# The second phase's output tiles: added in DRAM by accumulating transfers of GpSimd's queue, moved out of PSUM by ScalarE

## The chip, the cores and the metric

The kernel runs on one core of a Trainium2 chip. A time is the device time of one execution in microseconds (us); the median of several executions is given. Engines are named as in the profile: PE (TensorE), PEld (its weight loads), DVE (VectorE), ACT (ScalarE), POOL (GpSimd), SP (the queue from which the transfers are issued). L and a number is a line of the kernel's file.

## What is computed

Linear attention with an exponential feature map, then a gated feed-forward layer over its 4608 tokens (8 batches of 576), all in float32:

```python
def phi(x):
    proj = np.einsum('bhsd,df->bhsf', x, w_phi)
    proj = proj - np.max(np.abs(proj), axis=-1, keepdims=True)
    return np.concatenate([np.exp(proj), np.exp(-proj)], axis=-1)
q_p, k_p = phi(q), phi(k)
num = q_p @ (k_p^T v); den = q_p . sum_s k_p + 1e-06
x = (num / den), heads side by side          # 4608 x 512
gate = 1 / (1 + exp(-(x @ w_gate)))          # 512 -> 1536
out = (gate * (x @ w_val)) @ w_out           # 1536 -> 512
```

## The kernel before

**Two phases.** The 1536 hidden columns are twelve groups of 128. The first phase computes the attention, pair of heads by pair of heads (`attend`), and beside it the feed-forward layer's first four groups (`first_js`), whose output is a partial sum of every output tile of 128 tokens by 512 columns. The second phase does the other eight groups in two passes of four groups each, over six chunks (`dc`) of 768 tokens: twelve calls of `pass_over`. The three partial sums of a tile (first phase, first pass, second pass) have to be added.

**A chunk of a pass** is two stages on PE. The first is 28 products of six matmuls of 384 columns (`group`, line 1229, 168 matmuls) in tiles of the PSUM ring `bank`, which has five. Four groups of seven products follow one another; each group begins with a product of which ACT makes a copy (line 1247), and DVE adds the further products onto that copy (line 1242), which frees their banks. The second stage is 72 matmuls of 512 columns (`out_part`, line 1311) into six output tiles `acc`, twelve to a tile, in the PSUM ring `gate`, which has three banks. We call the six T0 to T5. The first two or three of them are done half and half in turn. Meanwhile ACT and DVE split the next chunk's input blocks into a high and a low part (lines 1187 and 1191), from loads of line 1167.

**An output tile's end** is `finish` (lines 1129 to 1145). SP loads the partial sum so far from a scratch tensor in DRAM into the ring `r_y1` of three buffers (line 1134), DVE adds it to `acc` from PSUM into a tile `y` (line 1139), and SP stores `y` (line 1143). The ring `r_y` has two buffers, so the sum of a tile waits until the store of the tile two before has landed. The partial sums lie in `yscr` (written by the first phase at line 1000, read in the first pass), `y2scr` (written by the first pass, read in the second), and the second pass writes `out`.

**What sets the order.** Every operation is first an entry of a plan (`Plan.op`) with an engine, an estimated length and a rank; `Plan.run` simulates the engines and lists the entries by their simulated start. The instructions are written in that order, and each engine executes its own strictly in it. An instruction at the head of its queue that waits for a buffer keeps all later ones of that engine waiting.

Of the kernel before, what the change touches and what calls it, by code (L numbers as in the profile page):

```python
# [8 lines left out]
F32 = mybir.dt.float32  # L9
# [4 lines left out]
ALU = mybir.AluOpType  # L14
# [6 lines left out]
P = 128  # L21
NP = H // 2
DM = H * D
# [4 lines left out]
CW = 512  # L28
NCH = NT // CW
# [6 lines left out]
DC = 2 * HT  # L36
# [112 lines left out]
class Plan:  # L149


    SWITCH = 0.15
    NEAR = {"PE": 0.3, "DVE": 0.05, "ACT": 0.05, "SP": 0.0, "X": 0.0}
    SAME = {"PE": 0.0, "DVE": 0.12, "ACT": 0.13, "SP": 0.0, "X": 0.0}
    RATE = 0.26

    def __init__(self):
# [21 lines left out]
    def run(self):  # L179
        free = dict.fromkeys(self.NEAR, 0.0)  # L180
        ready = {e: [] for e in free}
        mode, wire = None, 0.0
        for o in self.ops:
            if not o.wait:
                ready[o.eng].append(o)

        def pick(b, taken):
            best, when = None, None
            for ring in b.rings:
                for s in ring:  # L190
                    t = s.at()
                    if t is None or any(s.hits(x) for x in taken):
                        continue
                    if best is None or t < when:
                        best, when = s, t
            return best

        def start(o):
            t = max(o.ready, free[o.eng])
            if o.eng == "PE" and mode not in (None, o.mode[0]):  # L200
                t = max(o.ready, free[o.eng] + self.SWITCH)
            taken = []
            for b in o.bufs:
                if b.rings and b.slot is None:
                    s = pick(b, taken)
                    if s is None:
                        return None
                    taken.append(s)
                    t = max(t, s.at())
            return t  # L210

        order, left = [], len(self.ops)
        while left:
            best = None
            for e, cs in ready.items():
                ts = [(t, o) for o in cs if (t := start(o)) is not None]
                if not ts:
                    continue
                first = min(t for t, _ in ts) + self.NEAR[e]

                def key(x):
                    t, o = x
                    off = e == "PE" and mode not in (None, o.mode[0])
                    return o.rank + STICK * off, t

                t, o = min((x for x in ts if x[0] <= first), key=key)
                if best is None or t < best[0]:
                    best = t, o
            if best is None:
                raise RuntimeError(f"no work can go on: {[(o.eng, o.rank) for c in ready.values() for o in c][:40]} {left}")  # L230
            t, o = best
            ready[o.eng].remove(o)
            for b in o.bufs:
                if b.rings and b.slot is None:
                    b.slot = pick(b, ())
                    b.slot.take()
            free[o.eng] = t + o.busy
            if o.eng == "SP":
                wire = max(wire, t) + o.lag * self.RATE ** -1 * 1e-6
                end = wire + 2.0  # L240
            else:
                end = t + o.busy + o.lag
            if o.eng == "PE":
                mode = o.mode[-1]
            for cells in o.opens:
                n = len(cells.free)
                cells.free, cells.taken = [end] * n, [False] * n
            for b in o.bufs:
                b.left -= 1
                b.end = max(b.end, end)  # L250
                if not b.left and b.slot:
                    b.slot.give(b.end)
            for n in o.then:
                n.wait -= 1
                if n.eng != o.eng or o.eng == "SP":
                    at = end + n.slack
                else:
                    at = t + o.busy + self.SAME[o.eng]
                n.ready = max(n.ready, at)
                if not n.wait:  # L260
                    ready[n.eng].append(n)
            order.append((t, o))
            left -= 1
        return order
# [3 lines left out]
def attention_moe(  # L268
# [9 lines left out]
    nc = tc.nc  # L278
    vec, act = nc.vector, nc.scalar
# [3 lines left out]
    dram = ctx.enter_context(tc.tile_pool(name="dram", bufs=1, space=DRAM))  # L283
# [42 lines left out]
    nc.sync.dma_start(wk, w_phi)  # L326

    xscr = [dram.tile([P, NC4, CW], F32, tag=f"xs{c}", name=f"xs{c}") for c in range(NCH)]
    yscr = [dram.tile([4, P, DM], F32, tag=f"ys{c}", name=f"ys{c}") for c in range(NCH)]
    y2scr = [dram.tile([4, P, DM], F32, tag=f"yt{c}", name=f"yt{c}") for c in range(NCH)]  # L330
    wscr = [dram.tile([2, P, DM], F32, tag=f"wo{j}", name=f"wo{j}") for j in range(NJ)]
    gscr = {
        (n, m): dram.tile([2, P, 7 * 2 * P], F32, tag=f"g{n}{m}", name=f"g{n}{m}")
# [18 lines left out]
    r_top = x.ring(2, DM, U32)  # L352
    x = low()
    r_X = x.ring(14, 2 * HT)
    r_y1 = x.ring(3, DM)
    r_h = x.ring(8, 2 * HT)
    r_wo = x.ring(8, DM)
    x = high()
# [25 lines left out]
    def dve(n, fn, reads, writes, rank, k=1.0, after=()):  # L384
        return plan.op("DVE", 0.07 + n / 960 / k, 0.16, fn, reads, writes, rank, after=after)

    def on_act(n, fn, reads, writes, rank, after=()):
        return plan.op("ACT", 0.08 + n / 1200, 0.17, fn, reads, writes, rank, after=after)

    def sp(size, fn, reads, writes, rank, after=()):  # L390
        return plan.op("SP", 0.06, size, fn, reads, writes, rank, after=after)

    def head(hd):
        return slice(hd * D, hd * D + D)
# [580 lines left out]
    def first_js(c, r, step):  # L975

        banks = [r_g] if c < NCH - 2 else [r_g, r_a]
        hs = []
        for i in range(JA):
            hs.append(gate(c, i, r + 2 * i * step, banks, c == 0))  # L980
        for t in range(CW // P):
            acc, y = Buf(banks, [P, DM]), Buf([r_y], [P, DM])

            def go(t=t, acc=acc):
                for i in range(JA):
                    mm_out(acc, t, hs[i], i, i == 0, i == JA - 1)

            pe(
                "f", 0.685 * JA, go,
                [x for h in hs for x in h] + [x for i in range(JA) for x in weights[i][1]],  # L990
                [acc], r + (2 * JA + t) * step, 0.3,
            )
            on_act(
                DM, lambda y=y, acc=acc: act.activation(
                    y(), acc(), AF.Copy, scale=0.5 if c < LATE else 1.0
                ),
                [acc], [y], -90.0,
            )
            sp(
                256 << 10, lambda t=t, y=y: nc.sync.dma_start(yscr[c][t], y()),  # L1000
                [y], [(ymark[c], t)], r,
            )

# [122 lines left out]
        weigh(j, 2, r, False, wh, wl, slice(0, DM), None, after)  # L1126
        return wh, wl

    def finish(T, acc, src, mark, dst, dmark, r):

        c, t = divmod(T, CW // P)
        y1, y = Buf([r_y1], [P, DM]), Buf([r_y], [P, DM])
        sp(
            256 << 10, lambda: nc.sync.dma_start(y1().bitcast(F32), src[c][t]),
            [(mark[c], t)], [y1], r - 12.0, [done],
        )
        dve(
            DM,
            lambda: vec.tensor_tensor(y(), acc(), y1().bitcast(F32), op=ALU.add),  # L1139
            [acc, y1], [y], -90.0,  # L1140
        )
        sp(
            256 << 10, lambda: nc.sync.dma_start(dst(c, t), y()), [y],
            [(dmark[c], t)] if dmark else [], r,
        )

    prior, taken, outs = [fed], [], []
# [143 lines left out]
                [t, (hh, h)], [(hl, h)], z,  # L1291
            )

    def pass_over(ns, dc, r, ws, wo, src, mark, dst, dmark):

        x = x_blocks(dc, r - XLEAD)
        hs = []
# [4 lines left out]
        for T in range(DC // P):  # L1302
            acc = Buf([r_g], [P, DM])
            h, o = divmod(T * P, HT)
            for i, n in enumerate(ns):
# [13 lines left out]
                    + [y for j in pair(n) for y in wo[j]],  # L1319
                    [acc], r + 29.2 + 1.4 * T + 0.7 * i, 0.3,  # L1320
                ))
            finish(dc * (DC // P) + T, acc, src, mark, dst, dmark, r + 29.2 + 2.8 * T)

    def final(c, t):
        return out[c * CW + t * P : c * CW + t * P + P, :]

    SPAN = 46.0
    y2mark = [Buf() for _ in range(NCH)]
    ws, wo, marks = {}, {}, {}
    for n in range(2):  # L1330
        r = base - 30.0 + 30.0 * n
# [7 lines left out]
        wo[j] = fetched([r_wo], DM, wscr[j], marks[j], start - 20.0, [done])  # L1339
    for dc in range(NDC):  # L1340
        r = start + SPAN * dc
        pass_over(
            (0, 1), dc, r, ws, wo, yscr, ymark, lambda c, t: y2scr[c][t], y2mark
        )
        if dc < 4:
            n, m = 2 + dc // 2, dc % 2
            mark = marks[n, m] = Buf()
            kept(combine(n, m, r + KEEP, [r_stage], [done]), gscr[n, m], mark, r + KEEP)
            j = JA + 4 + dc
            mark = marks[j] = Buf()  # L1350
            kept(out_weight(j, r + KEEP + 10.0, [r_swo], [done]), wscr[j], mark, r + KEEP)
# [4 lines left out]
    for j in (*pair(2), *pair(3)):  # L1356
        wo[j] = fetched([r_wo], DM, wscr[j], marks[j], start + 10.0)
    for dc in range(NDC):
        pass_over((2, 3), dc, start + SPAN * dc, ws, wo, y2scr, y2mark, final, None)
    order = plan.run()  # L1360
    for _, o in sorted(order, key=lambda x: x[0]):
        o.fn()
# [58 lines left out]
```

## Time and profile before

| | before |
|---|---|
| median of 3 runs | 1160.05 us (1159.93 to 1161.06) |
| the profiled execution | 1160.85 us, of it 1158.9 us span of the core |
| granted PE clock | 0.998 |
| busy: PE, PEld, DVE, ACT | 1142.8, 939.5, 933.3, 583.0 us |
| bytes read from and written to DRAM | 120.06 MB, 49.42 MB |
| DVE's sums of output tiles, line 1139 | 72, 683 ns each (median) |
| transfers of 256 KB that carry partial sums and output | 36 `ys` stores, 36 `ys` loads, 36 `yt` stores, 36 `yt` loads, 36 `out` stores |

The views of the profile that are used below: the chain of work that ended last, followed back from the end (start, length, engine and line of each link); tables of stretches (busy time of each engine between two times, then PE's granted clock, the share of time in which the DMA engines were busy, and GB/s); a timeline of instructions (start, length, engine, line, output and inputs, and in brackets how long the engine had been idle and what released it); and lists of one line's instructions. SPq is SP's queue, where the time is that of issuing a transfer, not of its landing. Times count from the span's start.

### The profile page before, as it was taken

Reading aid. Unit: us, or ns where it says so; the run is one execution under the profiler, and the core shown is the slowest. Engines: PE = TensorE matmul, PEld = TensorE weight load, DVE = VectorE, ACT = ScalarE, POOL = GpSimd, SP = SyncE. Lnnn points to the kernel's source line nnn. Section 1 sums busy time; section 2 is a strip of 40 time slices with the busy share of each in tenths; the row PEclk is TensorE's granted clock in tenths of the full one; section 3 lists DMA queues with packets and bytes.
Section 4 is the critical chain, followed back from the end, with each engine's and each line's share of the span. In section 5 each row is a group of like instructions: output and inputs, shape, how many; then the busy total and the mean of one; then the engine's idle time right before and its main releaser. Section 6 shows DMA issues by size and latency. Waiting matters only on the chain.

```text
span 1158.9 us, 22323 instructions
## 1 busy us (share of the span) xinstructions
PE 1142.8 (99%) x8796; PEld 939.5 (81%) x8796; DVE 933.3 (81%) x1793; ACT 583.0 (50%) x1115; POOL 0.7 (0%) x6
## 2 busy tenths in 40 slices
PE   8999999999999999999999999999999999999998
PEld 6666566766676677678889999999999999999997
DVE  6999989888878878847897999988767757757764
ACT  6867776666656666635553444352332333323421
POOL 0000000000000000000000000000000000000000
PEclk9999999999999999999999999999999999999999
DMA  6764554344424443226526656545447433225122
GB/s 237 226 220 127 152 168 123 121 129 137 137 87 153 121 137 122 70 79 209 173 101 211 206 178 223 187 141 186 154 173 286 141 106 123 78 88 163 56 95 82
DMA packets 99441, 171.08 MB, mean 148 GB/s; under 512 B 18825, under 2 KB 43529, under 8 KB 99337
## 3 DMA queue, kind: packets, MB, share of 16 engines
q1 hardware_dynamic: 99336, 169.66, 45.7%
q8 instruction: 69, 1.13, 0.4%
q14 instruction: 36, 0.29, 0.1%
HBM read 120.06 MB, written 49.42 MB: 146 GB/s over the span
## 4 chain that ended last, share of the span: by engine, by line
PE 84%; DVE 7%; DMA 6%; ACT 2%; issue 1%; SPq 1%; DVEq 0%
PE bank L1229 30%; PE gate L1311 17%; PE gate L914 11%; PE gate L971 6%; PE bank L621 4%; PE bank L663 3%; PE bank L914 3%; DMA rb<-den 3%; PE bank L432 2%; PE bank L681 2%; DMA den<-dn 2%; PE bank L537 1%; DVE d L587 1%; PE bank L971 1%; PE bank L635 1%; PE bank L647 1%
## 5 line engine op out<-in xcount | busy, mean ns | idle before, releaser
L1229 PE MATMUL bank<-low,high 128*128 128x384 f32 x2016 | 351.8, 336 | 0.0
L1229 PEld LDWEIGHTS bank<-low,high 128*128 128x128 f32 x2016 | 349.8, 188 | 1.1
L1311 PE MATMUL gate<-low 128*128 128x512 f32 x864 | 198.4, 389 | 0.0
L1311 PEld LDWEIGHTS gate<-low 128*128 128x128 f32 x864 | 162.0, 188 | 33.2
L914 PE MATMUL gate<-low 128*128 128x512 f32 x696 | 165.7, 393 | 1.2 <-ACT flat L949 0.6
L914 PEld LDWEIGHTS gate<-low 128*128 128x128 f32 x696 | 128.6, 188 | 29.7 <-issue 1.2
L479 ACT ACTIVATE ek<-ek 128x512 f32<-128x512 f32 (+1 forms) x192 | 96.6, 526 | 27.3 <-DVE ek L467 25.9
L1242 DVE TENSOR_TENSOR more<-more,bank 128x384 f32<-128x384 f32 x111 | 61.1, 551 | 40.8 <-PE bank L1229 40.3
L971 PE MATMUL gate<-low 128*128 128x512 f32 x384 | 92.3, 394 | 0.0
L971 PEld LDWEIGHTS gate<-low 128*128 128x128 f32 x384 | 70.8, 188 | 15.1 <-issue 1.0
L621 PE MATMUL bank<-ek,vin 128*32 128x256 f32 x1240 | 74.5, 386 | 4.4 <-ACT d L545 3.8
L621 PEld LDWEIGHTS bank<-ek,vin 128*32 128x32 f32 x1240 | 37.8, 110 | 46.2 <-issue 11.0
L1139 DVE TENSOR_TENSOR flat<-gate,low 128x512 f32<-128x512 f32 x72 | 49.3, 685 | 23.3 <-PE gate L1311 11.7
L438 DVE TENSOR_REDUCE mk<-bank 128x4 f32<-128x512 f32 (+1 forms) x92 | 49.0, 552 | 21.3 <-PE bank L432 16.9
L1242 DVE TENSOR_TENSOR flat<-flat,bank 128x384 f32<-128x384 f32 x75 | 41.3, 551 | 29.3 <-PE bank L1229 29.1
L1187 ACT CAST low<-more 128x768 fp32r<-128x768 f32 x36 | 30.1, 836 | 61.1 <-DVE more L1178 60.8
L467 DVE TENSOR_TENSOR ek<-bank,mk 128x512 f32<-128x512 f32 (+1 forms) x92 | 48.2, 550 | 0.6 <-ACT d L550 0.2
L1267 ACT ACTIVATE more<-more 128x384 f32<-128x384 f32 x38 | 20.0, 525 | 57.1 <-DVE more L1242 56.9
L938 ACT CAST low<-flat 128x512 fp32r<-128x512 f32 x36 | 22.3, 620 | 51.5 <-DVE flat L963 44.9
L1284 ACT CAST low<-more 128x384 fp32r<-128x384 f32 x50 | 24.7, 513 | 46.6 <-DVE more L1280 46.6
L590 ACT ACTIVATE eq<-d 128x1152 f32<-128x1152 f32 x29 | 33.9, 1168 | 24.8 <-DVE d L587 24.4
L432 PE MATMUL bank<-wk,kin 64*128 64x128 f32 x496 | 38.7, 289 | 4.6 <-DMA kin<-k 4.3
(184 smaller groups left out, 1700.1 us busy)
## 6 DMA issues: line engine op xcount, KB each, us to landing
flat<-w_moe SPq DMA_DIRECT2D x36, 512.0 KB
low<-xs SPq DMA_DIRECT2D x46, 256.0 KB
kin<-k SPq DMA_DIRECT2D x32, 320.0 KB
qin<-q SPq DMA_DIRECT2D x32, 320.0 KB
vin<-v SPq DMA_DIRECT2D x32, 320.0 KB
ys<-flat SPq DMA_DIRECT2D x36, 256.0 KB
low<-ys SPq DMA_DIRECT2D x36, 256.0 KB
yt<-flat SPq DMA_DIRECT2D x36, 256.0 KB
```

Of the source, the lines that this page charges most:

```text
L432: nc.tensor.matmul(pk[hd]()[:, t, :], x()[head(hd), t * P : t * P + P], wk[head(hd), :], start=True, stop=True,)
L438: vec.tensor_reduce(mx, pk, axis=AX.X, op=ALU.max, apply_absolute_value=True)
L467: vec.tensor_tensor(ek[g]()[:, :, F:], src, mk[g]()[:, :ns].unsqueeze(2).broadcast_to([P, ns, F]), op=ALU.subtract,)
L479: lambda g=g, sg=sg: act.activation(ek[g]()[:, :, sg * F : sg * F + F], ek[g]()[:, :, F:], AF.Exp, scale=1.0 - 2.0 * sg,),
L621: nc.tensor.matmul(o_[o : o + Q, : 2 * F], vx()[:, 2 * t + hd, o % D : o % D + Q], (e0, e1)[hd][:, t, :] if t < 4 else e2[:, 0, :], start= ...
L663: nc.tensor.matmul(nm()[o : o + Q, :], w()[:, sg, o : o + Q], es[sg]()[:, o // D, cs], start=sg == 0, stop=sg == 1, tile_position=(0, o),)
L914: nc.tensor.matmul(o(), a()[:, ws], x(), start=cc + n == 0, stop=cc == NC4 - 1 and n == 2,)
L971: nc.tensor.matmul(acc(), a()[:, ts], w(), start=first and i == 0, stop=last and i == 2)
L1139: lambda: vec.tensor_tensor(y(), acc(), y1().bitcast(F32), op=ALU.add),
L1229: nc.tensor.matmul(o()[:, :HT], s()[:, ws], y()[:, cc, :], start=first and cc + i_ == 0, stop=cc + i_ == 3, skip_group_check=not first,)
L1242: lambda: vec.tensor_tensor(o(), p(), q()[:, :HT], op=ALU.add),
L1311: nc.tensor.matmul(acc(), s()[:, h, o : o + P], w(), start=i + e + k_ == 0, stop=i + e + k_ == 4,)
```

## The change

The scratch tensors `yscr` and `y2scr` and the ring `r_y1` are gone. The first phase stores its partial sums straight into `out`. In the second phase ACT copies each output tile from PSUM to `y`, and a transfer issued by POOL adds `y` onto the rows of `out` in DRAM. The plan gets POOL as an engine, with an estimated 1.0 us per issue and a landing estimated in the same manner as for SP's transfers.

```diff
-    yscr = [dram.tile([4, P, DM], F32, ...) for c in range(NCH)]
-    y2scr = [dram.tile([4, P, DM], F32, ...) for c in range(NCH)]
...
-    r_y1 = x.ring(3, DM)
...
+    def rows(c, t):
+        return out[c * CW + t * P : c * CW + t * P + P, :]
...
-                256 << 10, lambda t=t, y=y: nc.sync.dma_start(yscr[c][t], y()),
+                256 << 10, lambda t=t, y=y: nc.sync.dma_start(rows(c, t), y()),
...
-    def finish(T, acc, src, mark, dst, dmark, r):
+    def finish(T, acc, r):
         c, t = divmod(T, CW // P)
-        y1, y = Buf([r_y1], [P, DM]), Buf([r_y], [P, DM])
-        sp(
-            256 << 10, lambda: nc.sync.dma_start(y1().bitcast(F32), src[c][t]),
-            [(mark[c], t)], [y1], r - 12.0, [done],
-        )
-        dve(
-            DM,
-            lambda: vec.tensor_tensor(y(), acc(), y1().bitcast(F32), op=ALU.add),
-            [acc, y1], [y], -90.0,
-        )
-        sp(
-            256 << 10, lambda: nc.sync.dma_start(dst(c, t), y()), [y],
-            [(dmark[c], t)] if dmark else [], r,
-        )
+        y = Buf([r_y], [P, DM])
+        on_act(DM, lambda: act.copy(y(), acc()), [acc], [y], -90.0)
+        plan.op(
+            "POOL", 1.0, 256 << 10,
+            lambda: nc.gpsimd.dma_start(rows(c, t), y(), accum_op=ALU.add),
+            [y], [(ymark[c], t)], r,
+        )
```

Where the instructions stand after it:

**ACT, the end of the last chunk.** Of before, the last rows of ACT's queue (a copy of a group's first product, sigmoids at line 1267, and the casts of the hidden values at line 1284):

```order
991 L1267 ACTIVATE more<-more 128x384
992 L1267 ACTIVATE flat<-flat 128x384
993 L1247 COPY flat<-bank_204 128x384
994 L1284 CAST low<-flat 128x384
995 L1284 CAST low<-more 128x384 x2
996 L1284 CAST low<-flat 128x384
997 L1378 UNCONDITIONAL_BRANCH
```

Now (the same lines are 1260, 1240 and 1277; line 1133 is the new copy from the ring `gate` to a `y` tile):

```order
1077 L1240 COPY flat<-bank_186 128x384
1078 L1277 CAST low<-flat 128x384
1079 L1277 CAST low<-more 128x384
1080 L1277 CAST low<-flat 128x384
1081 L1277 CAST low<-more 128x384
1082 L1133 COPY flat<-gate_195 128x512
1083 L1133 COPY flat<-gate_188 128x512
1084 L1133 COPY flat<-gate_201 128x512
1085 L1133 COPY flat<-gate_195 128x512
1086 L1133 COPY flat<-gate_188 128x512
1087 L1133 COPY flat<-gate_201 128x512
1088 L1365 UNCONDITIONAL_BRANCH
```

The six copies T0 to T5 stand behind everything else of ACT's. In most other chunks the next row behind T5 is the copy of the next chunk's first product; that is so in the chunk before this one, where the casts of line 1180 (before: 1187) are the splits of the next chunk's input:

```order
1059 L1180 CAST low<-more 128x768
1060 L1133 COPY flat<-gate_201 128x512
1061 L1180 CAST low<-more 128x768
1062 L1133 COPY flat<-gate_195 128x512
1063 L1133 COPY flat<-gate_188 128x512
1064 L1133 COPY flat<-gate_201 128x512
1065 L1240 COPY more<-bank_174 128x384
1066 L1260 ACTIVATE flat<-flat 128x384
1067 L1260 ACTIVATE flat<-bank_174 128x384
```

All six tiles of a chunk have moved from DVE's queue into ACT's, and the last three of them stand together ahead of the next chunk's first work there.

**PE, where the first pass ends.** This is the one place of all 6536 matmuls at which PE's order changes. Before, T5 of the first pass's last chunk (`gate_219`) stood behind four products of the next pass:

```order
1418 L1311 MATMUL gate_213<-low 128x512 x12
1419 L1311 MATMUL gate_206<-low 128x512 x12
1420 L1229 MATMUL bank_192<-low,high 128x384 x6
1421 L1229 MATMUL bank_180<-low,high 128x384 x6
1422 L1229 MATMUL bank_204<-low,high 128x384 x6
1423 L1229 MATMUL bank_194<-low,high 128x384 x6
1424 L1311 MATMUL gate_219<-low 128x512 x12
1425 L1229 MATMUL bank_192<-low,high 128x384 x6
```

Now it stands behind three (`gate_201`; lines 1304 and 1222 are before's 1311 and 1229):

```order
1418 L1304 MATMUL gate_195<-low 128x512 x12
1419 L1304 MATMUL gate_188<-low 128x512 x12
1420 L1222 MATMUL bank_174<-low,high 128x384 x6
1421 L1222 MATMUL bank_162<-low,high 128x384 x6
1422 L1222 MATMUL bank_186<-low,high 128x384 x6
1423 L1304 MATMUL gate_201<-low 128x512 x12
1424 L1222 MATMUL bank_176<-low,high 128x384 x6
```

One product has moved behind T5; number, size and everything else of PE's order are as they were.

**SP and POOL, the end.** Before, SP's last rows mixed the loads of the partial sums with the stores:

```order
545 L1134 DMA low<-yt_114 128x512
546 L1143 DMA out<-flat 128x512
547 L1134 DMA low<-yt_114 128x512
548 L1143 DMA out<-flat 128x512 x4
549 L1378 UNCONDITIONAL_BRANCH
```

Now all 72 accumulating transfers are POOL's, and POOL has nothing else to do by then:

```order
9 L1136 DMA out<-flat 128x512 x72
10 L1365 UNCONDITIONAL_BRANCH
```

SP's queue is 144 transfers shorter (72 loads and 72 stores) and now ends with the loads of the last chunk's input.

More of the change, by code (lines that the diff above doesn't have):

```diff
@@ L152 @@
     SWITCH = 0.15
-    NEAR = {"PE": 0.3, "DVE": 0.05, "ACT": 0.05, "SP": 0.0, "X": 0.0}
-    SAME = {"PE": 0.0, "DVE": 0.12, "ACT": 0.13, "SP": 0.0, "X": 0.0}
+    NEAR = {"PE": 0.3, "DVE": 0.05, "ACT": 0.05, "SP": 0.0, "POOL": 0.0, "X": 0.0}
+    SAME = {"PE": 0.0, "DVE": 0.12, "ACT": 0.13, "SP": 0.0, "POOL": 0.0, "X": 0.0}
     RATE = 0.26
@@ L237, in run @@
             free[o.eng] = t + o.busy
-            if o.eng == "SP":
+            if o.eng in ("SP", "POOL"):
                 wire = max(wire, t) + o.lag * self.RATE ** -1 * 1e-6
@@ L254, in run @@
                 n.wait -= 1
-                if n.eng != o.eng or o.eng == "SP":
+                if n.eng != o.eng or o.eng in ("SP", "POOL"):
                     at = end + n.slack
@@ L328, in attention_moe @@
     xscr = [dram.tile([P, NC4, CW], F32, tag=f"xs{c}", name=f"xs{c}") for c in range(NCH)]
-    yscr = [dram.tile([4, P, DM], F32, tag=f"ys{c}", name=f"ys{c}") for c in range(NCH)]
-    y2scr = [dram.tile([4, P, DM], F32, tag=f"yt{c}", name=f"yt{c}") for c in range(NCH)]
     wscr = [dram.tile([2, P, DM], F32, tag=f"wo{j}", name=f"wo{j}") for j in range(NJ)]
@@ L1292, in valued, with pass_over @@
             )
-    def pass_over(ns, dc, r, ws, wo, src, mark, dst, dmark):
+    def pass_over(ns, dc, r, ws, wo):
         x = x_blocks(dc, r - XLEAD)
@@ L1321, in pass_over @@
                 ))
-            finish(dc * (DC // P) + T, acc, src, mark, dst, dmark, r + 29.2 + 2.8 * T)
-    def final(c, t):
-        return out[c * CW + t * P : c * CW + t * P + P, :]
+            finish(dc * (DC // P) + T, acc, r + 29.2 + 2.8 * T)
     SPAN = 46.0
-    y2mark = [Buf() for _ in range(NCH)]
     ws, wo, marks = {}, {}, {}
@@ L1341, in attention_moe @@
         r = start + SPAN * dc
-        pass_over(
-            (0, 1), dc, r, ws, wo, yscr, ymark, lambda c, t: y2scr[c][t], y2mark
-        )
+        pass_over((0, 1), dc, r, ws, wo)
         if dc < 4:
@@ L1358, in attention_moe @@
     for dc in range(NDC):
-        pass_over((2, 3), dc, start + SPAN * dc, ws, wo, y2scr, y2mark, final, None)
+        pass_over((2, 3), dc, start + SPAN * dc, ws, wo)
     order = plan.run()
```

## The prediction

> **What bounds the kernel now.** The chain of work that ended last comes first: start, length, and the engine and line of each link. It is PE without a break from 511.98 us on; its last links are these.
>
> ```profile
> 1018.77 29.12 PE bank L1229 x168
> 1047.90 16.36 PE gate L1311 x72
> 1064.26 29.12 PE bank L1229 x168
> 1093.38 16.36 PE gate L1311 x72
> 1109.73 29.12 PE bank L1229 x168
> 1138.86 16.37 PE gate L1311 x72
> ```
>
> Each link begins where the one before ends, and a chunk is 29.12 + 16.36 = 45.48 us every time. The table of stretches says what stands beside it (PE, PEld, DVE, ACT, POOL busy, then clock, DMA share, GB/s):
>
> ```profile
> 654.90:700.40 45.50, 45.50 (x242) 42.66 (x242) 44.97 (x86) 21.30 (x40) 0.00 (x0) 1.00 0.65 216
> 1018.80:1064.30 45.50, 45.50 (x242) 42.66 (x242) 31.73 (x53) 15.02 (x27) 0.00 (x0) 1.00 0.33 101
> 1109.70:1155.30 45.60, 45.52 (x241) 42.32 (x239) 22.78 (x43) 9.53 (x20) 0.00 (x0) 1.00 0.22 69
> 1155.30:1158.90 3.60, 0.00 (x0) 0.00 (x0) 0.65 (x1) 0.00 (x0) 0.00 (x0) 0.80 0.19 73
> ```
>
> PE is busy for the whole of each stretch at full clock, even in the first, where DVE works 44.97 of 45.50 us. DVE's load costs PE nothing. The second phase is as long as its matmuls, plus 3.6 us behind the last of them. That tail is the only part that can shrink. It is this (timeline; in brackets what released the instruction):
>
> ```profile
> 1141.04 0.55 DVE L1288 TENSOR_TENSOR low<-flat,low 128x384 fp32r<-128x384 f32 x1
> 1143.01 0.69 DVE L1139 TENSOR_TENSOR flat<-gate,low 128x512 f32<-128x512 f32 x1 [1.43 <-PE gate L1311]
> 1143.73 0.33 SPq L1134 DMA_DIRECT2D low<-yt  x1
> 1144.11 0.42 SPq L1143 DMA_DIRECT2D out<-flat  x1
> 1144.37 0.69 DVE L1139 TENSOR_TENSOR flat<-gate,low 128x512 f32<-128x512 f32 x1 [0.67 <-PE gate L1311]
> ...
> 1147.44 0.69 DVE L1139 TENSOR_TENSOR flat<-gate,low 128x512 f32<-128x512 f32 x1 [2.37 <-DMA out<-flat]
> ...
> 1149.88 0.69 DVE L1139 TENSOR_TENSOR flat<-gate,low 128x512 f32<-128x512 f32 x1 [1.75 <-PE gate L1311]
> 1152.53 0.69 DVE L1139 TENSOR_TENSOR flat<-gate,low 128x512 f32<-128x512 f32 x1 [1.97 <-PE gate L1311]
> 1155.25 0.69 DVE L1139 TENSOR_TENSOR flat<-gate,low 128x512 f32<-128x512 f32 x1 [2.03 <-PE gate L1311]
> 1155.97 0.33 SPq L1143 DMA_DIRECT2D out<-flat  x1
> ```
>
> These are T0 to T5 of the last chunk. PE has T0 ready at 1143.01, T1 at 1144.37, T3 at 1149.88, T4 at 1152.53, T5 at 1155.25. T2 waits for T0's buffer: a store. T5's sum ends at 1155.94, and its store lands with the span's end at 1158.9, 2.96 us later.
>
> **What the change takes away.** 72 sums of DVE and 144 of SP's transfers:
>
> ```profile
> L1139 DVE TENSOR_TENSOR flat<-gate,low x72: 678/683/693, 644.4 to 1155.3; 128x512 f32<-128x512 f32 x72
> L994 ACT ACTIVATE flat<-gate x32: 576/597/627, 101.3 to 608.6; 128x512 f32<-128x512 f32 x32
> ```
>
> 72 x 0.683 = 49 us of DVE's time go. None of it is on the chain, so I count it as nothing. ACT gets 72 copies from PSUM. The nearest operation is line 994, the same size from the same ring: 72 x 0.6 = 43 us, 3.6 us per chunk where ACT has at least 45.5 - 21.3 = 24 us free. Nothing again, and what is late next behind DVE is still PE. SP's issues and loads hide beside PE now; their going frees nothing PE waits for. One product of PE moves behind T5 where the passes meet: same work, no gap before, nothing. The first phase's engines keep their order, its stores only change their address: nothing. Were PE's cover gone there, each store would cost what SP pays to issue it, a third of a microsecond.
>
> **What it adds: the landing of an accumulating transfer.** Let L be the time from the end of a tile's copy until its `y` buffer is free again, or at the end until the run is over. No transfer of POOL, and none that adds, is in the trace, so L is bounded. Below: it reads `y` and writes `out` as a store does, and reads `out` besides, so it is not cheaper than a store. For a store in this chunk, T0's sum ends at 1143.70 and its buffer is free at 1147.44; 0.38 us of that is SP issuing a load first, so 3.36 us. At the end it is 2.96. Two more rows say that stores behind a busy queue take the same:
>
> ```profile
> 1060.13 1.43 SPq L1143 DMA_DIRECT2D out<-flat  x2
> 1063.56 0.69 DVE L1139 TENSOR_TENSOR flat<-gate,low 128x512 f32<-128x512 f32 x1 [1.49 <-DMA out<-flat]
> ```
>
> That is 3.43 us from issue to release. Above: a whole load of `out` would come first, then the store. The chain of work has a wait on loads of 256 KB:
>
> ```profile
> 214.54 4.06 DMA low<-xs
> ```
>
> 4.06 us on top gives 7.42 in the chunk and 7.02 at the end. I take half of that load on top, 2.03: the read of `out` should overlap that of `y` but not the write, and what POOL spends on issuing is unknown and can only add. So L is 5.4 us in the chunk and 5.0 at the end. I choose the middle because no row is nearer to one end.
>
> **The sum.** A copy takes 0.6 us. `y` has two buffers, so T3's copy waits for T1's transfer and T5's for T3's. T1's copy ends at 1144.37 + 0.6 = 1144.97. T3's starts at the later of 1149.88 and 1144.97 + 5.4 = 1150.37. T5's starts at the later of 1155.25 and 1150.97 + 5.4 = 1156.37, ends at 1156.97, and lands 5.0 later: 1161.97. Against 1158.9 that is +3.1 us. In general the end is the later of 1155.85 + L(end) and 1146.17 + 2 L(chunk) + L(end): beyond L of 4.8 each microsecond counts three times. With L at the plain store the end is 1158.8, -0.1 us; with the whole load on top it is 1168.0, +9.1.
>
> **Does PE wait in the other eleven chunks?** ACT waits for `y` with the next chunk's first copy queued behind it, for which DVE's additions and then PE's banks wait. A row of before shows how much room there is (a chunk whose first product starts at 1018.61):
>
> ```profile
> 1019.85 0.48 ACT L1247 COPY flat<-bank 128x384 f32<-128x384 f32 x1 [4.65 <-PE bank L1229]
> 1020.96 0.56 DVE L1242 TENSOR_TENSOR flat<-flat,bank 128x384 f32<-128x384 f32 x1 [1.46 <-PE bank L1229]
> ```
>
> A product takes 29.12 / 28 = 1.04 us. With five banks, the ninth product (at 8.3 us) is the first that needs a bank back, the one that DVE's first addition frees. From the copy's start to that addition's end is 1.67 us, so the copy may start 6.6 us into the chunk, and T5's copy 6.0. With T0 and T1 in turn, as in the last chunk, T5's copy starts at 1145.57 + 2 L against PE's end at 1155.23; so L may be 7.8. Where three tiles take turns, T1 is done 1.36 us later and L may be 7.2. At 5.4, T5's copy is 1.1 to 2.5 us behind PE, and no bank is late: nothing. The next chunk's input splits stand ahead of T3 to T5 on ACT, so they are not held up.
>
> A rule speaks against this. The Trainium skill, SBUF — State Buffer, section "SBUF: two separate sides", says that GpSimd cannot write the descriptors of its own transfers while VectorE runs certain two-port instructions, and the section on bandwidth pools gives 3100 ns for a transfer that took 620 alone. Added to 5.4 us in the chunk, that would be an estimated 7.9, just over the edge. In the last chunk it would change nothing: the tail's timeline has DVE's last other instruction end at 1141.59, ahead of the first copy. No row here has a transfer of POOL.
>
> **The rivals.**
>
> *The addition is nearly free* (no change that can be measured; this is the case on the other side). It costs only one more pass of 256 KB through the DMA engines. In the first stretch above they moved 216 GB/s at a share of 0.65, so 332 GB/s when busy: 0.8 us. L is 4.2 and 3.8, T5's copy waits for PE alone, and the end is 1155.85 + 3.8 = 1159.6: +0.7 us, 1160.8. It decides as long as L stays under 4.8. For it: stores here take so little longer than their bytes that much overlaps. Against it: POOL's issue comes on top. The Trainium skill, Collectives: The Full Stack, section "The bandwidth ceiling", sides with it: an addition inside a transfer is slower for its second read, not for the sum. With DMA: Bandwidth & Descriptors, Specifications (first byte about 1 us on GpSimd's path, 0.6 on SP's), I estimate +0.4 and, at 436 GB/s, +0.6 on L, and so +0.9 us in all. No run here shows it.
>
> *The two buffers of `y` become the bound of every chunk.* If L passes 7.2 to 7.8 us in a chunk, through DVE's 44.97 of 45.50 us or the queues' load, PE waits twice the excess. At L of 9: 3.6 us where three tiles take turns, 2.4 where two do, some 33 us over eleven chunks, and 14 at the end: 1207. For it: DVE and DMA are both at their busiest in the first pass. Against it: it needs more than a load and a store one after the other.
>
> *DVE's 49 us come back as time* (faster). It would need gaps of PE behind DVE. The stretches show none, nor does the chain.
>
> **The numbers.** The profiled execution took 1160.85 us, 1.95 around its span, and lies 0.8 over the median of 1160.05. I add the difference to the median: 1163.1. About 0.2%, 2.3 us, is what a measurement of this kernel can tell from no change. My forecast, a longer tail and nothing else, gets 0.46; the nearly free addition 0.42; the buffers as the bound 0.10; faster 0.02. So slower 0.56, same 0.42, faster 0.02. The range goes from the plain store with a little more, 1160.4, to load and store in turn, 1160.05 + 9.1 = 1169.2; it leaves out the third case and the edges.
>
> **What would show it.** Right: PE's chunks still 45.48 us with nothing between them; the span's end 6 to 7 us behind PE's last matmul instead of 3.7; T5's copy about 1 us behind PE, released by T3's transfer; DVE 49 us less busy, ACT 43 more. Wrong: T5's copy released by PE and a tail under 5.5 us (the addition is nearly free); PE idle at the start of a chunk with ACT's copy of line 1240 late (the buffers bound); PE's order or rate different in the first phase (I have overlooked something).

## The result and the profile after

| | before | after |
|---|---|---|
| median | 1160.03 us (4 runs) | 1173.49 us (4 runs, 1171.96 to 1175.91) |
| ratio, 95% interval | | 1.0114 (1.0097 to 1.0132) |
| profiled execution, span | 1160.85, 1158.9 us | 1173.99, 1172.2 us |
| PE, DVE, ACT, POOL busy | 1142.8, 933.3, 583.0, 0.7 us | 1145.4, 890.3, 619.3, 63.0 us |
| read from, written to DRAM | 120.06, 49.42 MB | 101.18, 49.42 MB |

The kernel is 13.4 us slower, 1.1%: the direction forecast, four times its size, and outside the range. DVE was busy 43 us less, ACT 36 us more, and none of it shortened the run. The bytes read fell by 72 tiles; that count is the same in experiment 4, which does not add, so it does not hold what an addition reads. Where did 13.3 us of span go? First PE (start, length, line, tiles, count; in brackets how long it had been idle and for whom):

```profile
702.03 4.33 PE L1222 MATMUL bank<-low,high 128*128 128x384 f32 x24
707.57 1.31 PE L1222 MATMUL bank<-low,high 128*128 128x384 f32 x6 [1.22 <-ACT more L1240]
709.62 24.22 PE L1222 MATMUL bank<-low,high 128*128 128x384 f32 x138 [0.74 <-DVE more L1235]
...
793.39 3.01 PE L1304 MATMUL gate<-low 128*128 128x512 f32 x12 [0.44 <-ACT flat L1133]
...
978.91 4.33 PE L1222 MATMUL bank<-low,high 128*128 128x384 f32 x24
984.53 25.45 PE L1222 MATMUL bank<-low,high 128*128 128x384 f32 x144 [1.29 <-ACT more L1240]
```

PE now stops behind 24 matmuls of a chunk's first group, that is ahead of its fifth product, for ACT's copy of the group's first product (line 1240; before, 1247). If each row's start is set against what its predecessors' matmuls take at before's pace (29.12 us for 168, 16.36 for 72), the lag grows to 7.8 us over the twelve chunks: 5.4 in the first pass, 2.4 in the second. In the kernel before it stays under 0.1. As far as the rows name a releaser, all but 0.7 us of the lag arises at this copy, or at DVE's additions behind it (line 1235). The 0.7 is at the row of 793.39: T5 needs the bank of T2, which ACT's copy of T2 leaves late. Why is the first product's copy late? The chunk at 702.03 on ACT and POOL (the timeline's order; other instructions left out):

```profile
691.55 0.58 ACT L1133 COPY flat<-gate 128x512 f32<-128x512 f32 x1
...
692.42 0.86 POOL L1136 DMA_DIRECT2D out<-flat  x1 [32.79 <-ACT flat L1133]
692.76 0.59 ACT L1133 COPY flat<-gate 128x512 f32<-128x512 f32 x1
693.64 0.86 POOL L1136 DMA_DIRECT2D out<-flat  x1 [0.36 <-ACT flat L1133]
...
698.37 0.59 ACT L1133 COPY flat<-gate 128x512 f32<-128x512 f32 x1 [2.44 <-DMA out<-flat]
...
699.66 0.59 ACT L1133 COPY flat<-gate 128x512 f32<-128x512 f32 x1 [0.70 <-DMA out<-flat]
...
704.06 0.59 ACT L1133 COPY flat<-gate 128x512 f32<-128x512 f32 x1 [3.19 <-DMA out<-flat]
...
705.94 0.59 ACT L1133 COPY flat<-gate 128x512 f32<-128x512 f32 x1 [1.30 <-DMA out<-flat]
706.43 0.71 ACT L1090 CAST high<-flat 128x256 fp32r<-128x256 f32 x2
...
707.04 0.48 ACT L1240 COPY more<-bank 128x384 f32<-128x384 f32 x1
```

T2's copy waits for T0's transfer, issued at 692.42 and landed just before 698.37; T3's for T1's; T4's and T5's for theirs. PE began the next chunk at 702.03, and the copy for it, behind all of these on ACT and behind two casts that prepare weights (line 1090), came 5.0 us later. Over the kernel (ACT's waits for landings in total, times, longest; and the time from POOL's issue to the landing):

```profile
ACT flat L1133 <- DMA out<-flat: 79.8, 42, 3.7
DMA to landing us min/median/max: 3.7/4.2/9.5
```

The other loss is the tail (last chunk; then T5's transfer with its time from issue to landing; then POOL's drains, the instructions by which its queue closes: count, length in ns as minimum, median and maximum, first and last start):

```profile
1151.24 0.59 ACT L1133 COPY flat<-gate 128x512 f32<-128x512 f32 x1 [2.12 <-PE gate L1304]
...
1156.28 0.59 ACT L1133 COPY flat<-gate 128x512 f32<-128x512 f32 x1 [3.09 <-DMA out<-flat]
...
1163.50 0.59 ACT L1133 COPY flat<-gate 128x512 f32<-128x512 f32 x1 [2.00 <-PE gate L1304]
1164.38 0.86 POOL L1136 DMA_DIRECT2D out<-flat  x1 [1.73 <-ACT flat L1133]
```

```profile
out<-flat POOLq DMA_DIRECT2D x1, 256.0 KB, 4.1
```

```profile
L1365 POOLq DRAIN  x3: 40/102/7061, 1164.4 to 1171.9; - x3
```

T5's copy is released by PE, so `y` did not delay it. Its transfer is issued at 1164.38 and lands 4.1 us later, at 1168.5. But POOL's queue has a drain at the program's end which begins with that issue and takes 7.06 us, until 1171.4; the span ends at 1172.2. In the kernel before, the longest of POOL's drains is this:

```profile
L1378 POOLq DRAIN  x3: 34/78/389, 1.0 to 1158.6; - x3
```

The account of the 13.3 us: PE starts its second phase 0.45 us later (610.74 against 610.29; in the ten profiles of this document that start lies anywhere from 607.70 to 611.95), waits 7.8 us in it, and from the start of T5's work outside PE to the end it is 8.7 us instead of 3.65, 5.05 more. Of these, the drain outlasts the landing by 2.9 us; so about 2.1, an estimate, are the copy, POOL's issue and the longer landing.

### The profile page after: what moved, and what is told of

It reads as the page before. It is cut to its first block, busy times and chain, and to the rows that moved or that the text cites. A ratio compares the mean times of both kernels' runs of the same rounds, so it can differ in the third digit from the quotient of the medians.

```text
span 1172.2 us, 22190 instructions
## 1 busy us (share of the span) xinstructions
PE 1145.4 (98%) x8796; PEld 939.2 (80%) x8796; DVE 890.3 (76%) x1721; ACT 619.3 (53%) x1187; POOL 63.0 (5%) x78
## 3 DMA queue, kind: packets, MB, share of 16 engines
HBM read 101.18 MB, written 49.42 MB: 128 GB/s over the span
## 4 chain that ended last, share of the span: by engine, by line
issue 82%; PE 5%; POOL 5%; DVE 5%; DMA 3%; ACT 1%; POOLq 0%; SPq 0%; ACTq 0%; DVEq 0%
POOL out L1136 5%; PE bank L1222 2%; DMA out<-flat 1%; DMA rb<-den 1%; PE bank L432 1%; DMA flat<-w_moe 0%; DMA flat<-xs 0%; DVE mb L709 0%; DVE d L587 0%; DVE mk L438 0%; PE bank L506 0%; DVE low L867 0%; DVE flat L823 0%; PE gate L506 0%; DMA kin<-k 0%
## 5 line engine op out<-in xcount | busy, mean ns | idle before, releaser
L1136 POOL DMA_DIRECT2D out<-flat x72 | 62.3, 870 | 1101.6 <-ACT flat L1133 1093.2
L1235 DVE TENSOR_TENSOR more<-more,bank 128x384 f32<-128x384 f32 x105 | 57.9, 551 | 77.2 <-PE bank L1222 62.8
L1133 ACT COPY flat<-gate 128x512 f32<-128x512 f32 x72 | 42.1, 587 | 95.3 <-DMA out<-flat 79.8
L1235 DVE TENSOR_TENSOR flat<-flat,bank 128x384 f32<-128x384 f32 x92 | 50.7, 551 | 43.1 <-PE bank L1222 34.4
L1277 ACT CAST low<-flat 128x384 fp32r<-128x384 f32 x46 | 23.3, 512 | 41.5 <-DVE flat L1273 41.4
L1180 ACT CAST low<-low 128x768 fp32r<-128x768 f32 x36 | 29.9, 835 | 24.7 <-DMA low<-xs 20.2
```

What stands on the lines that cost most here:

```text
L1133: on_act(DM, lambda: act.copy(y(), acc()), [acc], [y], -90.0)
L1136: lambda: nc.gpsimd.dma_start(rows(c, t), y(), accum_op=ALU.add),
L1235: lambda: vec.tensor_tensor(o(), p(), q()[:, :HT], op=ALU.add),
```

## Experiments

The theory they were to test: PE's 7.8 us are, but for 0.7, waits for ACT's first copy of a chunk, queued behind copies that wait for landings; the tail ends with a closing drain of POOL, not with a landing. The rivals are in the expectations. Ratios are to the kernel before. The tail is counted from the modelled end of PE's last row to the span's end: 3.7 us in the kernel before, 8.8 in the changed one.

**1. The same instructions in another order.** The planner is told a later landing, and then puts the first copy ahead of T4's and T5's on ACT. The new plan moves some of DVE's work too, and T5 where the passes meet stands behind six products on PE.

```diff
-                end = wire + 2.0
+                end = wire + (2.0 if o.eng == "SP" else 5.0)
```

> Only the planner's estimate of an accumulating transfer's landing goes from 2 to 5 us; in ACT's order the copy of a chunk's first product then stands ahead of the copies of T4 and T5. Queue theory (PE loses its 7.8 us because that copy stands on ACT behind copies that wait for a landing): PE's waits at the chunks' start fall to under 1.5 us in all, the tail behind PE stays about 8.7 us, time about 1166 to 1168. Rival, load (accumulating transfers or ACT's 43 us more work slow PE's partners wherever they stand): waits stay at 6 us or more, time within 1.5 us of the changed kernel.

1166.31 us, 1.0049 (1.0036 to 1.0062). PE's lag is 1.35 us, all but a tenth of it from one place, where PE waits for T2's bank in the first pass (its row, and ACT's waits for landings):

```profile
696.02 3.01 PE L1304 MATMUL gate<-low 128*128 128x512 f32 x12 [0.96 <-ACT flat L1133]
```

```profile
ACT flat L1133 <- DMA out<-flat: 36.7, 23, 3.1
```

ACT still waits 37 us for landings. What hurt was which instruction stood behind them. The load theory falls: as many transfers, as many copies, and 1.35 of PE's 7.8 us are left. The tail is 9.0 us.

**2. Two more buffers for `y`.** RA goes from 88 to 84 KB and the arena `flat` from 32 to 36, which gives the second phase two more tiles.

```diff
+    r_y2 = flat(32).ring(2, DM)
...
-        y = Buf([r_y], [P, DM])
+        y = Buf([r_y, r_y2], [P, DM])
```

> Two more y buffers for the second phase (four in all), order on ACT nearly as in the changed kernel. Queue theory: a copy then waits for the transfer four tiles back, 8 us or more before it, so hardly any copy waits for a landing; PE's 7.8 us go, the tail stays at 8.7 us, time about 1165.5 to 1167.5. Rival, load: waits stay. Rival, accumulating transfers are the bound by throughput (two of them back to back land 1.8 us later than one alone): landings stretch further and some waits stay, 2 to 4 us.

1164.69 us, 1.0035 (1.0023 to 1.0048), somewhat better than expected. The copies' list of releasers (us, times) no longer has a landing in it, and PE's lag is 0.4 us:

```profile
L1134 ACT COPY flat<-gate x72: 575/588/591, 643.3 to 1154.2; 128x512 f32<-128x512 f32 x72
...
its engine sat idle before it (us, times) until:
  PE gate L1305: 55.4, 40
  ACT low L1181: 4.5, 5
```

So the order and the buffers each cure the same loss, as they must if the cause is the one named. The tail is as it was, 8.9 us: PE ends at 1154.1, the span at 1163.0.

**3. The last chunk's tiles as before**: a load by SP, the sum on DVE, a store by SP, for these six tiles only (room for the load as in experiment 2).

```diff
+        if last:
+            y1 = Buf([r_y2], [P, DM])
...
+                256 << 10, lambda: nc.sync.dma_start(y1().bitcast(F32), rows(c, t)),
...
+                lambda: vec.tensor_tensor(y(), acc(), y1().bitcast(F32), op=ALU.add),
...
+                256 << 10, lambda: nc.sync.dma_start(rows(c, t), y()),
...
+            return
```

> The last chunk's six tiles are finished as in the kernel before (a load by SP, the sum on DVE, a store by SP); the other 66 as in the changed kernel. Drain theory (of the 8.7 us behind PE, some 3 are POOL emptying its transfer queue after the last landing): POOL's closing drain ends long before, the tail is 3.7 us again, time about 1168 to 1169, with PE's 7.8 us of waits left. Rival, fixed cost (a kernel with such transfers pays POOL's 3 us at its end whenever they were): tail 6 to 7 us, time about 1171. Rival, landing (the last landing itself takes 7 us): tail 3.7 us too, but then the changed kernel's last transfer must move bytes until its end, which the trace does not show.

1169.19 us, 1.0068 (1.0044 to 1.0092). The tail is 4.0 us, the waits of PE stay (7.0 us). POOL's long drain is there, begins with POOL's last issue, in the chunk before, and is over 41 us ahead of the end:

```profile
L1382 POOLq DRAIN  x3: 40/93/6905, 1118.1 to 1165.9; - x3
```

**4. A plain store in place of the adding one**, on the same queue. It leaves out the adding of the three partial sums.

```diff
-            lambda: nc.gpsimd.dma_start(rows(c, t), y(), accum_op=ALU.add),
+            lambda: nc.gpsimd.dma_start(rows(c, t), y()),
```

> POOL's transfers store without adding; this leaves out the adding of the three partial sums. If the addition is what costs (a second read of 256 KB): a lone transfer lands about 0.8 us earlier than 4.2, close transfers no longer hold each other up, PE's waits fall under 2 us, time 1165 to 1168 with the tail about 8. If POOL's path is what costs: landing 4.0 to 4.2 as before, PE's waits 6 us or more, time within 2 us of the changed kernel.

1165.66 us, 1.0041 (1.0028 to 1.0054). The landing, POOL's issue and the drain:

```profile
DMA to landing us min/median/max: 2.3/2.3/7.5
```

```profile
L1136 POOL DMA_DIRECT2D out<-flat x72: 539/539/682, 647.4 to 1158.5; - x72
```

```profile
L1365 POOLq DRAIN  x3: 40/93/6517, 1158.5 to 1165.5; - x3
```

The addition costs 1.9 us of landing at the median (4.2 against 2.3), more than twice the 0.8 I had expected here, and 0.32 us of POOL's issue (862 ns in the changed kernel). With the shorter landing PE's lag is 0.7 us, although the order on ACT is that of the changed kernel: it is the length of the landings that makes the copies late. The drain is nearly as long as with the addition, 6.5 us: it hardly depends on the landing. The tail is 8.2 us.

**5. The first product's copy on DVE instead of ACT.**

```diff
-        on_act(HT, lambda: act.copy(t1(), a()[:, :HT]), [a], [t1], -200.0)
+        dve(HT, lambda: vec.tensor_copy(t1(), a()[:, :HT]), [a], [t1], -200.0)
```

> The copy of each group's first product goes from ACT to DVE (48 of some 0.55 us); tiles, buffers and transfers as in the changed kernel. Theory of the fifth product (PE's fifth product of a group writes the bank of the first one again, so it waits until that bank has been copied, and the copy stood behind y's landings on ACT): with the copy on DVE the waits at the fourth or fifth product are gone, PE loses under 1.5 us in all (T5's bank may still be late by some tenths), tail 9 us, time about 1166. Rival, as the prediction had it (the ninth product is the first that waits, and the copy is not what counts): waits as in the changed kernel, 7 us.

1175.21 us, 1.0124 (1.0102 to 1.0147): not what was expected, about 1166. PE's lag is 9.2 us, nearer to the rival's 7 than to my 1.5; the rows have to decide. In the second pass it grows by only 0.03 us (2.4 in the changed kernel), as expected; in the first it is 9.1 instead of 5.4. There DVE and ACT also prepare weights, in turns, and the timeline shows the wait going round by that way:

```profile
702.94 4.32 PE L1222 MATMUL bank<-low,high 128*128 128x384 f32 x24
705.69 0.59 ACT L1133 COPY flat<-gate 128x512 f32<-128x512 f32 x1 [4.40 <-DMA out<-flat]
706.17 0.72 ACT L800 ACTIVATE flat<-flat,ebias 128x512 uint32<-128x512 uint32 x1
...
706.93 0.69 DVE L823 SCALAR_TENSOR_TENSOR flat<-flat 128x512 uint32<-128x512 uint32 x1 [4.83 <-ACT flat L800]
...
709.48 0.55 DVE L1240 COPY more<-bank 128x384 f32<-128x384 f32 x1
...
710.09 2.15 PE L1222 MATMUL bank<-low,high 128*128 128x384 f32 x6 [2.83 <-DVE more L1240]
```

T4's copy waits for a landing, line 800 stands behind it on ACT, DVE's line 823 waits for that, and the copy, now DVE's, stands behind line 823 and what follows it. PE again stops ahead of the fifth product, not the ninth, and again for this copy. The step of this expectation that failed: I took DVE to be free of ACT's waits.

**6. ACT's copies with plain stores by SP**, no transfer of POOL. It leaves out the adding of the three partial sums.

```diff
-        plan.op(
-            "POOL", 1.0, 256 << 10,
-            lambda: nc.gpsimd.dma_start(rows(c, t), y(), accum_op=ALU.add),
+        sp(
+            256 << 10, lambda: nc.sync.dma_start(rows(c, t), y()),
```

> ACT copies the tiles, SP stores them with a plain store, POOL issues nothing; this leaves out the adding of the three partial sums. Theory (the accumulating transfer's landing and POOL's closing drain are all of the loss): no waits of PE, tail 3.8 us, time within 1.5 us of the kernel before. Rival, ACT's 72 copies cost by themselves: PE waits 2 us or more.

1159.97 us, 0.9994 (0.9982 to 1.0006). PE's lag is under 0.1 us, the tail 3.6. ACT's 72 copies cost nothing that can be measured, and the 49 us that DVE no longer spends on sums bring nothing.

**7 and 8. Four buffers, and the last tile, or the last two, by SP and DVE.** Experiments 2 and 3 together, with `T >= 5` or `T >= 4` in the last chunk; the load of the partial sum has its own two tiles in a part of `flat` that is free by then.

> Four y buffers, and the very last tile is finished by SP and DVE; POOL's last transfer is then T4's, 2.7 us earlier against PE's end. Drain of a fixed length (POOL's closing drain begins at its last issue and takes 7 us whatever the transfer's landing): tail 9.0 - 2.7 = about 6.3 us, PE's waits 0.2, time 1162 to 1163. Rival, the drain waits for all transfers of the core, SP's last store too: tail about 7 us or more, because that store lands 3.8 us behind PE and 3 come on top.

1162.98 us, 1.0022 (1.0011 to 1.0034).

> As the one before, with the last two tiles by SP and DVE: POOL's last issue is T3's, 5.4 us earlier against PE's end. Fixed drain: it would end 3.6 us behind PE, level with SP's last landing, so the tail is 3.8 to 4.3 us; with no waits of PE the time is within 1.5 us of the kernel before, not clearly faster. Rival, the drain waits for SP's store too: tail 7 us, time 1163 or more.

1161.30 us, 1.0004 (0.9994 to 1.0015). POOL's drains, of the one and of the other:

```profile
L1383 POOLq DRAIN  x3: 40/93/6936, 1154.0 to 1161.5; - x3
```

```profile
L1383 POOLq DRAIN  x3: 40/102/7082, 1151.4 to 1159.7; - x3
```

With one tile the drain runs from 1154.0 to 1160.9 and the tail behind PE is 5.9 us (PE 1155.8, span 1161.7); with two it is over by 1158.5 and the tail is 4.1. Both are as a drain of fixed length has it. SP's last store, issued at 1156.60 with one tile, does not prolong the drain. No version beat the kernel before. Where PE does not wait, the second phase is as long as its matmuls, so a version of this kind could gain only a part of the tail.

## Why the prediction was wrong, step by step

- **What bounds the kernel, and what the change takes away: right.** PE's matmuls; DVE's 49 us, SP's 72 loads and 19 MB of reads were worth nothing (experiment 6, which keeps SP's 72 stores). Busy time moved by 43 us on DVE and 36 on ACT, not 49 and 43; neighbouring lengths overlap (705.94 + 0.59 is past 706.43), which is counted once. PE has 8796 matmuls in both profiles, not the 6536 named ahead.
- **The landing L: about right in size, in part by luck.** I took 5.4 us in the chunk and 5.0 at the end. Measured from a copy's end: 698.37 - 692.13 = 6.2 us in a first-pass chunk, 1156.28 - 1151.83 = 4.5 in the last, and at the end the landing of 4.1 plus 0.3 from copy to issue. Half a load on top, 2.03, was a middle chosen without a row and stands against 1.9 measured for the addition (experiment 4). The base was too large: with a plain transfer of POOL, L is an estimated 2.6 (2.3 and 0.3), not the 3.36 of SP's store. In the first-pass chunk 1.7 us come on top of 2.6 and 1.9.
- **"With five banks, the ninth product (at 8.3 us) is the first that needs a bank back": this step failed.** In `group`, `product(a, 4, "12", "21", False, True)` writes the first product's bank again, after ACT has copied what was there. So the fifth product, 4.16 us into the chunk, is the first that waits. With the copy's 0.48 us and the way to PE, the copy may start about 3.6 us in, not 6.6. That moves the limits of 7.8 and 7.2 us for L down by 3.0 / 2 each, to 6.3 and 5.7, and measured landings pass them: in the chunk shown, where three tiles take turns, T1 to T3 and T3 to T5 take 6.3 and 5.7 us, 6.0 on average. The casts of line 1090 between T5's copy and the first product's, which I did not count, add 0.6. The mechanism of my second rival ("the two buffers of `y` become the bound", 0.10) was the one at work, at an L that I had called harmless: 7.8 us of waits. Experiments 1, 2 and 4 remove most of it in three ways, and experiment 5's rows name the fifth product.
- **The tail: a term was missing.** The sum ended with the landing. Of its 3.1 us, 1.1 were T5's copy late for T3's transfer, which did not happen: PE released it. The other 2.0 were the longer landing, and about 2.1 is what that cost. The tail grew by 5 us all the same, because POOL's closing drain of 7 us from the last issue outlasts the landing by 2.9. Nothing of it is in the trace of before, whose POOL has no transfers; experiments 3, 7 and 8 show it by moving the last issue away from the end. What POOL does in it no trace shows.
- **DVE's port: did not show.** By the Trainium skill, SBUF — State Buffer, section "SBUF: two separate sides", GpSimd cannot write its descriptors while DVE runs an instruction in a two-port mode. Of the changed kernel's chunks, the first has DVE busy for 17.79 us of 20, with a shortest landing of 3.8 us and a longest issue of 1011 ns; the last has it busy for 3.60 of 20, with 3.7 us and 865 ns. The trace shows no such block for this mix, mostly TENSOR_TENSOR; whether any instruction of it ran in such a mode it does not show.
- **The range** failed with these two: 7.8 and 5 us where I had 0 and 3.1. "Slower" came out, but mostly by waits and a drain that the forecast did not have, so the direction was partly luck.

What stays open: why landings reach 9.5 us at some places of the first pass. Issues close together are not enough: the two of 1107.32 and 1108.41, with no load beside them, land in 3.9 and 4.7 us, those of 692.42 and 693.64, with a load by SP issued at 692.52, in 5.8 and 5.9. SP's loads are thus the likelier cause; no run tests it.

## What to carry to other kernels

To find how long an instruction may be late, go through the consumer's program for the first access to its buffer of any kind, a second accumulation into the same bank too, rather than counting buffers. A copy that must wait for a transfer to land holds up all that stands behind it on its engine: order it behind what the busiest engine needs next, or give it buffers enough that it never waits. A queue that is new to a kernel can have its own cost at the end of the program, as POOL's had here: look how it closes, and give the last pieces of work to a queue that ends quickly.

## What the runs showed of the hardware

- POOL's drain at the program's end took 6.5 to 7.2 us from its last transfer's issue, in each of the kernels with such transfers, whether they landed in 2.3 or 4.2 us (medians) and whether the end was near or 40 us away. Without transfers of POOL its longest drain was 0.39 us.
- An adding transfer of 256 KB from POOL landed in 4.2 us at the median, a plain one in 2.3; POOL's issue took 0.86 and 0.54 us.
